# Splitting the tokens' high and low parts over three steps, and the closing sums behind one convolution step

## Chip, cores and metric

One core of one Trainium2 chip. The time is device time in microseconds (us) of one launch; below it is the median of three runs of the kernel before. TensorE is PE (its weight loads are PEld), VectorE DVE, ScalarE ACT, GpSimd POOL, SyncE SP.

## The reference

A convolution whose seven taps are drawn per token and head by a softmax, and behind it a feed-forward layer with squared relu:

```python
w = exp(weight_gen - max(weight_gen, -1)); w = w / (sum(w, -1) + 1e-9)   # B S 8 7
x_pad = concatenate([zeros(6 rows), x], axis=1)                          # x: 8 x 4096 x 192
attn = einsum('bshk,bskhg->bshg', w, x_pad[:, s + k])                    # 24 columns a head
h = attn.reshape(32768, 192) @ w_in                                      # 192 x 2048
out = (maximum(h, 0) ** 2) @ w_out                                       # 2048 x 192
```

x and weight_gen are float32; w_in and w_out come as float64 and are decoded by the kernel.

## The kernel before, in words

**Tiling.** The 32768 tokens lie 256 to a partition; a chunk is 4 tokens of each partition, 512 tokens, so there are 64 chunks. For a chunk, DVE makes the softmax and the seven products and adds of the convolution (`conv_steps`, lines 326 to 500), turns the result with a 32 x 32 transpose (L487), and SP sends it through memory (`xr` to `xd` with four DMAs, L493, `xd` to `xT` with two, L498), so that the 192 columns stand on partitions. `xT` has three parts of 512 columns, one for each third of the 192.

**Precision.** PE multiplies in a reduced float32 form. Each operand is therefore split into a high part, rounded by a copy on ACT (`high_part`, L427, `xT` to `xh`; `high`, L550, `rg` to `gh`), and a low part, the rest, by a subtraction on DVE (`low_part`, L430, to `xl`; `low`, L559 and L562, to `gl`).

**Steps.** A chunk is worked in eight steps j (the loop at lines 878 to 932). In step j PE multiplies the tokens by 2 of the 16 column blocks of W (`mm1`, L522: nine products for each block, in the order xh for the three parts, xl for the three parts, xh with W's low part), ACT does relu (L539), square (L546) and the high half (L550), and DVE does the low half one step later (`late`). Two steps behind (LAG) PE multiplies the finished blocks by V (`mm2_scaled`, L603 and L607) into four PSUM banks. Every product is done in two halves of 64 rows, which PE's array runs side by side. After the last block of a chunk come 32 small products (L613), and the chunk's sums are closed: `sum_turned` copies one half's bank by ACT (L648) and adds the other half's by DVE (L650), part 0 and then part 1. Only then may the next chunk's L603 products write these banks. The closing of chunk c - 1 stands in step 1 of chunk c, its banks are wanted again in step 2.

**Chunks 6 to 62** are "scaled": x and V are scaled by powers of two, so that the low halves `gl` can be kept in float16 (`V16` is V's float16 copy, kept with part of `gl` in the tile `du`). The factors come from the peaks of W and V (`peak_w`, `peak_v`), which `spread_peaks` (lines 299 to 304) sends to memory and back to all partitions with two DMAs, and from which `coefficients` computes eight numbers. `scale_v` (lines 321 to 324) scales V in place.

**Order.** Each engine works its instructions in the order in which they are written here. `at(c, j, f)` puts f into the list `todo` of step j of chunk c; entries made before the loop stand first. The convolution of chunk m begins in step 1 of chunk m - 2: SCALED_SLOTS says how many of its 19 steps go to each of ten successive steps of the loop; the last, `turn`, falls in step 2 of chunk m - 1. The splits of chunk m are put into steps 5 and 6 of chunk m - 1 (lines 856 and 857). Where a step closes a chunk, N_AHEAD entries of its list come before the closing sums (lines 908 to 927). In step 1 the list holds the last product and the last add of the next chunk's convolution and the maximum and the subtraction of the softmax of the chunk after it.

Of the kernel before, what the change touches and what calls it, by code (L numbers as in the profile page):

```python
# [8 lines left out]
F32 = mybir.dt.float32  # L9
# [4 lines left out]
AF = mybir.ActivationFunctionType  # L14
ALU = mybir.AluOpType
# [15 lines left out]
def kernel(  # L31
# [9 lines left out]
    nc = tc.nc  # L41
    B, S, D = x.shape
# [3 lines left out]
    P = 128  # L46
# [10 lines left out]
    ND = D // D1  # L57
    N = TC * P
    NJ = NF // 2
# [3 lines left out]
    LAG = 2  # L63
    CONV_BEG = 1
    CONV_SLOTS = (2, 1, 4, 1, 3, 0, 3, 3, 0, 3)
    SCALED_SLOTS = (2, 1, 4, 1, 2, 1, 3, 2, 2, 1)
    OUT_STEP = 3
    LOAD_STEP = 5
    NBUF = NF // 2
    FIRST = 6  # L70
    GL_POOL = 5
    SCALE_STEP = NJ
    N_AHEAD = 2

    const = ctx.enter_context(tc.tile_pool(name="const", bufs=1))
    stage = ctx.enter_context(tc.tile_pool(name="stage", bufs=3))
# [33 lines left out]
    def is_scaled(c):  # L110
        return FIRST <= c < NCH - 1
# [7 lines left out]
    V = const.tile([P, NF, 2 * D], F32R, name="V")  # L119
    du = const.tile([P, 4, 2 * WI], U32, name="du")  # L120
    du_flat = du.rearrange("p a b -> p (a b)")
    V16 = du_flat[:, 0:NF * D // 2].bitcast(F16).rearrange("p (f e) -> p f e", f=NF)
# [3 lines left out]
    tops = du_flat[:, NF * D // 2:NF * D // 2 + 2 * P].bitcast(F32)  # L126
    coef = const.tile([P, 8], F32, name="coef")
    w_mul, v_mul, v_root, v_unroot = (coef[:, k:k + 1] for k in range(4))
# [39 lines left out]
    def load_rest():  # L168
        t0 = rows_of(0)
        wf = w_tiles[0].rearrange("p t h k -> p t (h k)")  # L170
        nc.sync.dma_start(out=wf[:, TC:, :], in_=wg_v[:, t0 + TC:t0 + TG, :])
        nc.sync.dma_start(out=x_tiles[0][:, HALO + TC:, :], in_=x_v[:, t0 + TC:t0 + TG, :])
# [73 lines left out]
    def dec(u, *idx, half=None):  # L246
        if u not in decs:
            decs[u] = decode_steps(u)
        i0, i1 = (0, 2) if half is None else (half, half + 1)
        for n in idx:  # L250
            decs[u](n, i0, i1)
            if n == 3 and i1 == 2 and u + 3 < 2 * NU:
                load_weights(u + 3)
                if u == 1:
                    load_rest()
# [43 lines left out]
    def spread_peaks():  # L299
        dm = dram.tile([P, 2], F32, name="dm")  # L300
        pk = coef[:, 4:6]
        nc.vector.tensor_reduce(out=pk, in_=peaks.rearrange("p (w k) -> p w k", w=2), axis=AX.X, op=ALU.max)
        nc.sync.dma_start(out=dm, in_=pk)
        nc.sync.dma_start(out=tops, in_=dm.rearrange("p w -> (p w)").rearrange("(o n) -> o n", o=1).broadcast_to([P, 2 * P]))

    def coefficients():
        ts = nc.vector.tensor_scalar
# [10 lines left out]
        ts(out=v_root.bitcast(U32), in0=v_root.bitcast(U32), scalar1=POW2, scalar2=None, op0=ALU.bitwise_and)  # L318
        nc.vector.tensor_tensor(out=v_mul, in0=v_root, in1=v_root, op=ALU.mult)

    def scale_v(j):
        v = V[:, 2 * j:2 * j + 2]
        nc.vector.tensor_scalar(out=v, in0=v.bitcast(F32), scalar1=v_mul, scalar2=None, op0=ALU.mult)
        nc.scalar.copy(V16[:, 2 * j:2 * j + 2], v[:, :, 0:D].bitcast(F32))

    def conv_steps(c, on_pe, moving=False):
        gi, lo = divmod(c, CPG)
# [2 lines left out]
        n = TC * H  # L330
# [74 lines left out]
        def both(*fs):  # L405
            return lambda: [f() for f in fs]
# [25 lines left out]
        def split(k):  # L432
            return both(lambda: high_part(k), lambda: low_part(k))

        splits = [split(k) for k in range(ND)]
        if moving and not on_pe:
            splits = [[lambda f=f, k=k: f(k) for k in range(ND)] for f in (high_part, low_part)]

# [109 lines left out]
    def high(c, fb):  # L548
        gh = ghs[c, fb] = gp.tile([P, N], F32R, name="gh")
        nc.scalar.copy(gh, rgs[c, fb])  # L550

    def low(c, fb):
        if is_scaled(c):
            j, i = divmod(fb, 2)
            if i == 0:
                gls[c, j] = gp.tile([P, 2, N], F16, name="gl") if j < GL_POOL else gl_rest[:, j - GL_POOL]
            gl = gls[c, j][:, i].rearrange("p (m i) -> p i m", i=2)
            g, h = (v.rearrange("p (i m) -> p i m", i=2) for v in (rgs.pop((c, fb)), ghs[c, fb].bitcast(F32)))
            nc.vector.tensor_tensor(out=gl, in0=g, in1=h, op=ALU.subtract)  # L559
            return  # L560
        gl = gls[c, fb] = gp.tile([P, N], F32R, name="gl")
        nc.vector.tensor_tensor(out=gl, in0=rgs.pop((c, fb)), in1=ghs[c, fb].bitcast(F32), op=ALU.subtract)  # L562
# [79 lines left out]
    def sum_turned(c, parts=(1, 0)):  # L642
        acc = accs[c]
        if c not in works:
            works[c] = stage.tile([P, 3, N], F32, name="raw")
        X = works[c]
        for k in parts:
            nc.scalar.copy(X[:, k], acc[2 * k])  # L648
        for k in parts:
            nc.vector.tensor_tensor(out=X[:, k], in0=acc[2 * k + 1], in1=X[:, k], op=ALU.add)  # L650
        if 1 in parts and is_scaled(c):
            nc.gpsimd.dma_start(out=X[0:D1, 1], in_=X[D1:P, 1], accum_op=ALU.add)  # L652
        elif 1 in parts:
            nc.sync.dma_start(out=X[0:D1, 2], in_=X[D1:P, 1])
# [57 lines left out]
    def store(c, t0, t1):  # L712
        put_out(c, t0, t1, outs[c][0], 1 if c == 0 else 0)
# [44 lines left out]
    done = iter(range(NF))  # L758
# [68 lines left out]
    todo, soon, pend, late = {}, {}, [], []  # L827

    def at(c, j, f):
        todo.setdefault((c + j // NJ, j % NJ), []).append(f)  # L830
# [5 lines left out]
    def plan_conv(m, a, b):  # L836
        if m == 3:
            for f in a[:2]:
                at(1, 1, f)
            soon[1, 2] = a[2:3]  # L840
            spread(a[3:], 1, 3, 3 + NJ)
        elif m > 3:
            fs = iter(a)
            for j, n in enumerate(SCALED_SLOTS if is_scaled(m) else CONV_SLOTS):
                for _ in range(n):
                    at(m - 2, CONV_BEG + j, next(fs))
        else:
            for j, fs in enumerate(((), a[4:5], a[5:8], a[8:])):
                for f in fs:
                    at(1, j, f)  # L850
        if m < 2 + CPG:
            soon[m - 1, NJ - 1] = b[0] + b[1][:ND * (m == 2)]
            for f in b[1][ND * (m == 2):]:
                at(m - 1, NJ - 1, f)
        else:
            for k, f in enumerate(b):
                at(m - 1, NJ - 3 if k == 0 and is_scaled(m) else NJ - 2, f)

    for k in range(4):
        at(2, k + 3, lambda k=k: peak_v(k))  # L860
        at(3, k, lambda k=k: peak_w(k))
    at(3, 4, spread_peaks)
    at(3, 7, coefficients)
    for j in range(NJ):
        at(FIRST - 1, j + 4, lambda j=j: scale_v(j))
    for gi in range(FIRST // CPG, NCH // CPG):
# [7 lines left out]
    plan_conv(3, *conv_steps(3, 0, True))  # L874
    for u in range(1, NU):
        at(1, 2 * u, lambda u=u: dec(NU + u, 5))

    for c in range(1, NCH):
        tail = c == NCH - 1
        for j in range(NJ):  # L880
            if j == (LOAD_STEP if c > 1 else 0) and c % 2 and (c + 3) // 2 * CPG < NCH:
                load_group((c + 3) // 2)
            if j == CONV_BEG and 1 < c < NCH - 2:
                plan_conv(c + 2, *conv_steps(c + 2, 0))
            if c == 1 and j == 0:
                mm1(c, j, (0, 1, 6, 7, 3, 4, 2, 8, 5), 5)
            else:
                mm1(c, j)
            fbs = (2 * j, 2 * j + 1)
            done = None  # L890
            if len(pend) == LAG or tail and pend:
                c2, j2 = pend.pop(0)
                for fb in (2 * j2, 2 * j2 + 1):
                    mm2_turned(c2, fb)
                done = c2 if j2 == NJ - 1 else None
            for f in soon.pop((c, j), []):
                f()
            for fb in fbs:
                relu(c, fb)
            for fb in fbs:  # L900
                square(c, fb)
            if not tail:
                pend.append((c, j))
            for f in late:
                f()
            late.clear()
            fs = todo.pop((c, j), [])
            split_sum = done is not None and is_scaled(done)
            if split_sum:
                for f in fs[:N_AHEAD]:  # L910
                    f()
                del fs[:N_AHEAD]
                sum_turned(done, (0,))
            elif done is not None:
                sum_turned(done)
            for f in fs:
                f()
            if c > 1:
                for part in range(2):
                    if j == (LOAD_STEP if tail else 2 * part + 2 if is_scaled(c - 1) else OUT_STEP + part):  # L920
                        store_turned(c - 1, part)
            if not tail or j < NJ // 2:
                for fb in fbs:
                    high(c, fb)
                    late.append(lambda c=c, fb=fb: low(c, fb))
            if split_sum:
                sum_turned(done, (1,))
            if c == 1 and j == 0:
                for t in range(TC // 2):
                    finish(0, t)  # L930
            if c == 1 and j == NJ - 1:
                store(0, 0, TC)
    c = NCH - 1
# [56 lines left out]
```

## Time and profile before

| | |
|---|---|
| median of 3 runs | 2102.3 us (2101.99 to 2102.64) |
| profiled execution | 2101.76 us |
| its span, first to last instruction | 2100.0 us |
| granted TensorE clock, mean | 0.998 of 2.4 GHz |
| busy | PE 2074.4, PEld 1707.0, DVE 1870.8, ACT 1845.2, POOL 221.2 us |

The profile is of one execution. A busy time counts the union of an engine's instructions; matmuls overlap each other, so PE's share says little of its peak. An idle time is put down to the instruction that released the engine.

### The profile page before, as it was taken

The numbers are of one execution on the slowest core, as the hardware profiler recorded it, in microseconds if no ns is written. First come the engines' busy times: TensorE is split into PE (matmuls) and PEld (weight loads), VectorE is DVE, ScalarE is ACT, GpSimd is POOL, SyncE is SP. The second block draws the span as 40 slices with busy tenths as digits, with TensorE's granted clock in tenths as the row PEclk, the third lists the DMA queues.
The fourth block names the chain that finished last, engine by engine and source line by source line (L and its number), as shares of the span: only waits on it lengthen the run. The fifth ranks groups of instructions, "written<-read, shape, count | busy, mean of one in ns | idle before, by whom it ended". The sixth has DMA issues, their size and how long they took to land.

```text
span 2100.0 us, 49532 instructions
## 1 busy us (share of the span) xinstructions
PE 2074.4 (99%) x19484; PEld 1707.0 (81%) x19484; DVE 1870.8 (89%) x2953; ACT 1845.2 (88%) x3551; POOL 221.2 (11%) x364
## 2 busy tenths in 40 slices
PE   9999999999999999999999999999999999999999
PEld 8887878878888788888888788787788878888878
DVE  9989899898898898998988988989889889999885
ACT  8887988889888899889898888998888988988986
POOL 0000110111110111101111101111011110011110
PEclk9999999999999999999999999999999999999999
DMA  9524454534545445445355354354453553544522
GB/s 234 101 51 98 108 117 97 122 73 105 125 97 110 93 91 118 113 98 121 70 110 126 94 113 93 90 120 106 104 120 71 110 125 93 116 85 97 122 59 56
DMA packets 322289, 217.78 MB, mean 104 GB/s; under 512 B 215696, under 2 KB 273168, under 8 KB 318216
## 3 DMA queue, kind: packets, MB, share of 16 engines
q1 hardware_dynamic: 300568, 181.17, 37.3%
q0 software_dynamic: 21488, 33.46, 9.4%
q8 instruction: 152, 2.49, 0.5%
q14 instruction: 81, 0.66, 0.1%
HBM read 106.52 MB, written 49.55 MB: 74 GB/s over the span
## 4 chain that ended last, share of the span: by engine, by line
PE 71%; DVE 15%; DMA 6%; ACT 4%; issue 2%; SPq 1%; DVEq 0%; ACTq 0%
PE ph L522 38%; PE acc L603 21%; DMA xT<-xd 4%; PE acc L607 4%; PE acc L613 4%; DVE pr L384 4%; DVE du L559 3%; DVE pr L397 3%; PE acc L638 3%; DVE xl L430 2%; DVE raw L650 1%; DVE gl L559 1%; ACT rg L539 1%; PE acc L570 1%; ACT rg L546 1%
## 5 line engine op out<-in xcount | busy, mean ns | idle before, releaser
L522 PE MATMUL ph<-xh,W 64*128 64x512 f32 x6096 | 1069.0, 403 | 0.0
L522 PEld LDWEIGHTS ph<-xh,W 64*128 64x128 f32 x6096 | 718.3, 186 | 100.9 <-ACT gh L550 23.0
L603 PE MATMUL acc<-gh,V 64*128 64x512 f32 x5472 | 772.9, 378 | 10.1 <-DVE raw L650 8.4
L539 ACT ACTIVATE rg<-ph 128x512 f32<-128x512 f32 x992 | 539.0, 596 | 197.8 <-PE ph L522 193.1
L603 PEld LDWEIGHTS acc<-gh,V 64*128 64x128 f32 x5472 | 594.4, 186 | 104.1 <-DVE raw L650 32.2
L546 ACT ACTIVATE rg<-rg 128x512 f32<-128x512 f32 x1007 | 580.5, 634 | 0.2
L550 ACT CAST gh<-rg 128x512 fp32r<-128x512 f32 x1008 | 576.1, 626 | 3.0 <-PE acc L580 3.0
L522 PE MATMUL ph<-xl,W 64*128 64x512 f32 x3048 | 495.3, 376 | 0.1
L559 DVE TENSOR_TENSOR gl<-rg,gh 128x512 f16<-128x512 f32 x570 | 389.6, 740 | 47.4 <-ACT gh L550 47.4
L384 DVE TENSOR_TENSOR pr<-xt,wt 128x768 f32<-128x768 f32 x440 | 412.3, 949 | 2.3
L522 PEld LDWEIGHTS ph<-xl,W 64*128 64x128 f32 x3048 | 361.5, 186 | 40.4 <-ACT xl L441 0.5
L397 DVE TENSOR_TENSOR pr<-pr 128x768 f32<-128x768 f32 x309 | 295.2, 955 | 6.1
L559 DVE TENSOR_TENSOR du<-rg,gh 128x512 f16<-128x512 f32 x342 | 232.0, 732 | 3.7 <-ACT gh L550 3.7
L607 PE MATMUL acc<-gl,du 64*128 64x512 f16 x1140 | 230.8, 381 | 1.0 <-DVE gl L559 1.0
L430 DVE TENSOR_TENSOR xl<-xT,xh 128x512 fp32r<-128x512 f32 x186 | 122.2, 687 | 122.0 <-ACT xh L427 121.8
L652 POOL DMA_DIRECT2D raw<-raw x57 | 47.3, 830 | 1261.3 <-DVE raw L650 1170.6
L607 PEld LDWEIGHTS <-du 64*128 64x128 f16 x1824 | 101.7, 95 | 62.3 <-issue 4.7
L607 PE MATMUL acc<-du 64*128 64x512 f16 x684 | 138.2, 382 | 0.0
L285 POOL DMA_DIRECT2D x_out<-x_fac x232 | 112.3, 493 | 42.5 <-DVE x_fac L282 41.4
L427 ACT CAST xh<-xT 128x512 fp32r<-128x512 f32 x186 | 108.1, 619 | 9.3 <-DMA xT<-xd 8.6
L402 POOL DMA_DIRECT2D pr<-pr x63 | 57.0, 905 | 531.3 <-DVE pr L384 484.8
L613 PEld LDWEIGHTS <-du 64*64 64x64 f16 x1824 | 48.3, 106 | 57.9 <-issue 24.1
(127 smaller groups left out, 1267.7 us busy)
## 6 DMA issues: line engine op xcount, KB each, us to landing
xT<-xd SPq DMA_DIRECT2D x124, 384.0 KB
xt<-in_x_dram SPq DMA_DIRECT2D x30, 1344.0 KB
out_dram<-o_sb SPq DMA_DIRECT2D x254, 96.0 KB
pr<-pr POOLq DMA_DIRECT2D x63, 384.0 KB, 5.8
xd<-xr SPq DMA_DIRECT2D x248, 96.0 KB
o_sb<-raw SPq DMA_DIRECT2D x342, 64.0 KB
raw<-raw POOLq DMA_DIRECT2D x57, 128.0 KB, 3.9
wt<-in_weight_gen_dram SPq DMA_DIRECT2D x31, 224.0 KB
```

Source lines behind the costliest of these rows:

```text
L285: nc.gpsimd.dma_start(out=fo[b * P // n:(b + 1) * P // n], in_=f[b::n])
L384: tt(out=dst, in0=src, in1=wf[:, t0 * H:t1 * H, k:k + 1].broadcast_to([P, m, G]), op=ALU.mult)
L397: tt(out=prs[k0], in0=prs[k0], in1=prs.pop(k), op=ALU.add)
L430: tt(out=parts["l"][:, k, n], in0=src[k][:, n], in1=parts["h"][:, k, n].bitcast(F32), op=ALU.subtract)
L522: nc.tensor.matmul(two[i], w, order(xx[rows, k]), start=(n == 0), stop=(n == last))
L539: nc.scalar.activation(r, ph, AF.Relu)
L546: nc.scalar.activation(r, r, AF.Square)
L550: nc.scalar.copy(gh, rgs[c, fb])
L559: nc.vector.tensor_tensor(out=gl, in0=g, in1=h, op=ALU.subtract)
L603: nc.tensor.matmul(acc[b + h], V[rows, fb, e:e + P], two_halves(g[rows]), start=fb == 0 and e < 2 * P, stop=False)
L607: nc.tensor.matmul(acc[h], V16[rows, 2 * j + i, 0:P], gls[c, j][rows, i], start=False, stop=last and i == 1)
L613: nc.tensor.matmul(acc[2 + h][i * D1:(i + 1) * D1], V16[rows, 2 * k + i, P:D], gls[c, k][rows, i], start=False, stop=k == NJ - 1, tile_pos ...
```

## The change

The splits of a scaled chunk m: in step 5 of chunk m - 1 the high parts 0 and 1, in step 6 the low parts 0 and 1 and the high part 2, in step 7 the low part 2 (before: high and low 0 in step 5, high and low 1 and 2 in step 6). SCALED_SLOTS moves convolution steps accordingly: step 5 takes one more, step 7 one less, and step 6 a product in place of an add. In a closing step of a scaled chunk one convolution step is ahead of the sums in place of two, and the two sums stand together, with only the high halves (ACT) between; the rest of the list follows. The DMAs of `spread_peaks` are issued by POOL two steps later, `coefficients` is three steps later, in chunk 4. V's float16 copies are made straight from the unscaled V in chunk 4, alternately on DVE and ACT, and the scaling in place in chunks 5 and 6 alternates likewise.

```diff
-    SCALED_SLOTS = (2, 1, 4, 1, 2, 1, 3, 2, 2, 1)
+    SCALED_SLOTS = (2, 1, 4, 1, 3, 1, 2, 2, 2, 1)
-    N_AHEAD = 2
+    N_AHEAD = 1
@@ spread_peaks
-        nc.sync.dma_start(out=dm, in_=pk)
-        nc.sync.dma_start(out=tops, in_=dm.rearrange(...).broadcast_to([P, 2 * P]))
+        nc.gpsimd.dma_start(out=dm, in_=pk)
+        nc.gpsimd.dma_start(out=tops, in_=dm.rearrange(...).broadcast_to([P, 2 * P]))
@@
+    def scaled_copy(j, o, i):
+        if j % 2:
+            nc.scalar.activation(o, i.bitcast(F32), AF.Copy, scale=v_mul)
+        else:
+            nc.vector.tensor_scalar(out=o, in0=i.bitcast(F32), scalar1=v_mul, scalar2=None, op0=ALU.mult)
+
+    def make_v16(j):
+        scaled_copy(j, V16[:, 2 * j:2 * j + 2], V[:, 2 * j:2 * j + 2, 0:D])
+
     def scale_v(j):
         v = V[:, 2 * j:2 * j + 2]
-        nc.vector.tensor_scalar(out=v, in0=v.bitcast(F32), scalar1=v_mul, scalar2=None, op0=ALU.mult)
-        nc.scalar.copy(V16[:, 2 * j:2 * j + 2], v[:, :, 0:D].bitcast(F32))
+        scaled_copy(j, v, v)
@@ conv_steps
+        if is_scaled(c):
+            splits = [(lambda k=k: high_part(k), lambda k=k: low_part(k)) for k in range(ND)]
@@ plan_conv
-            for k, f in enumerate(b):
-                at(m - 1, NJ - 3 if k == 0 and is_scaled(m) else NJ - 2, f)
+            for f in b if not is_scaled(m) else ():
+                at(m - 1, NJ - 2, f)
+            for k, (f, g) in enumerate(b if is_scaled(m) else ()):
+                at(m - 1, NJ - 3 + k // 2, f)
+                at(m - 1, NJ - 2 + k // 2, g)
@@
-    at(3, 4, spread_peaks)
-    at(3, 7, coefficients)
+    at(3, 6, spread_peaks)
+    at(4, 2, coefficients)
+    for j in range(NJ):
+        at(4, 3 + j // 2, lambda j=j: make_v16(j))
@@ the loop of steps
+            if split_sum:
+                highs_of(c, fbs)
+                sum_turned(done, (1,))
             for f in fs:
                 f()
...
-            if not tail or j < NJ // 2:
-                for fb in fbs:
-                    high(c, fb)
-                    late.append(lambda c=c, fb=fb: low(c, fb))
-            if split_sum:
-                sum_turned(done, (1,))
+            if not split_sum and (not tail or j < NJ // 2):
+                highs_of(c, fbs)
```

`highs_of` holds the loop over `high` and `late.append` that stood here.

## Rows read from the trace of the kernel before

**Rows 1.** The page: engines' busy time; line L430 (busy us, mean ns | idle before).

```profile
PE 2074.4 (99%) x19484; PEld 1707.0 (81%) x19484; DVE 1870.8 (89%) x2953; ACT 1845.2 (88%) x3551; POOL 221.2 (11%) x364
...
L430 DVE TENSOR_TENSOR xl<-xT,xh 128x512 fp32r<-128x512 f32 x186 | 122.2, 687 | 122.0 <-ACT xh L427 121.8
```

**Rows 2.** PEld in order of time (start us, us, instruction), chunks 62 and 63.

```profile
2035.32 0.51 PEld L522 LDWEIGHTS ph<-xh,W 64*128 64x128 f32 x6 [0.41 <-ACT gh L550]
...
2038.89 0.62 PEld L522 LDWEIGHTS ph<-xh,W 64*128 64x128 f32 x6
...
2061.00 0.62 PEld L522 LDWEIGHTS ph<-xh,W 64*128 64x128 f32 x6
...
2066.84 0.51 PEld L522 LDWEIGHTS ph<-xh,W 64*128 64x128 f32 x6 [0.41 <-ACT gh L550]
```

**Rows 3.** PEld in order of time, chunk 6 step 2 and chunk 7 step 3.

```profile
231.06 0.62 PEld L522 LDWEIGHTS ph<-xh,W 64*128 64x128 f32 x6
...
271.60 0.83 PEld L522 LDWEIGHTS ph<-xh,W 64*128 64x128 f32 x6
```

**Rows 4.** PEld in order of time, chunk 30, steps 1 to 3.

```profile
1000.98 0.83 PEld L522 LDWEIGHTS ph<-xh,W 64*128 64x128 f32 x6
...
1007.03 0.51 PEld L522 LDWEIGHTS ph<-xh,W 64*128 64x128 f32 x6 [0.41 <-ACT gh L550]
...
1009.88 0.73 PEld L603 LDWEIGHTS acc<-gh,V 64*128 64x128 f32 x7 [0.39 <-DVE raw L650]
...
1010.87 0.83 PEld L522 LDWEIGHTS ph<-xh,W 64*128 64x128 f32 x6
```

**Rows 5.** The waits view (engine line <- releaser: us in total, times, longest).

```profile
PEld acc L603 <- DVE raw L650: 32.2, 59, 1.0
...
DVE coef L309 <- DMA du<-dm: 9.0, 1, 9.0
...
ACT xh L427 <- DMA xT<-xd: 8.6, 22, 0.9
```

**Rows 6.** DVE in order of time, closings in chunk 30 and in chunk 62.

```profile
1006.95 0.96 DVE L397 TENSOR_TENSOR pr<-pr 128x768 f32<-128x768 f32 x1
...
1009.14 0.68 DVE L650 TENSOR_TENSOR raw<-acc,raw 128x512 f32<-128x512 f32 x1
...
1011.05 0.98 DVE L487 STREAM_TRANSPOSE xr<-pr 128x768 f32<-128x768 f32 x1
...
2036.04 0.69 DVE L650 TENSOR_TENSOR raw<-acc,raw 128x512 f32<-128x512 f32 x1 [0.60 <-ACT raw L648]
2036.65 1.38 DVE L559 TENSOR_TENSOR gl<-rg,gh 128x512 f16<-128x512 f32 x2
```

**Rows 7.** PEld and SP's queue in order of time, chunks 3 and 4.

```profile
151.21 0.64 PEld L522 LDWEIGHTS ph<-xh,W 64*128 64x128 f32 x6
...
165.45 0.62 PEld L522 LDWEIGHTS ph<-xh,W 64*128 64x128 f32 x6
...
149.93 0.54 SPq L303 DMA_DIRECT2D dm<-coef  x1
152.79 0.34 SPq L304 DMA_DIRECT2D du<-dm  x1
```

**Rows 8.** Groups of instructions by line: scaling and copying of V.

```profile
L323 DVE TENSOR_SCALAR V<-V,coef 128x768 fp32r<-128x768 f32 x8 | 4.9, 611 | 0.0
...
L324 ACT CAST du<-V 128x384 f16<-128x384 f32 x8 | 4.1, 510 | 4.6 <-DVE V L323 4.5
```

**Rows 9.** ACT and PEld in order of time, chunk 30 step 5 to chunk 31.

```profile
1022.66 0.62 ACT L427 CAST xh<-xT 128x512 fp32r<-128x512 f32 x1
...
1027.32 1.15 ACT L550 CAST gh<-rg 128x512 fp32r<-128x512 f32 x2
...
1029.94 0.83 PEld L522 LDWEIGHTS ph<-xl,W 64*128 64x128 f32 x6
```

**Rows 10.** The page's DMA issues: POOL's accumulating DMA (KB each, us to landing).

```profile
pr<-pr POOLq DMA_DIRECT2D x63, 384.0 KB, 5.8
```

More of the change, by code (lines that the diff above doesn't have):

```diff
@@ L302, in spread_peaks @@
         nc.vector.tensor_reduce(out=pk, in_=peaks.rearrange("p (w k) -> p w k", w=2), axis=AX.X, op=ALU.max)
-        nc.sync.dma_start(out=dm, in_=pk)
-        nc.sync.dma_start(out=tops, in_=dm.rearrange("p w -> (p w)").rearrange("(o n) -> o n", o=1).broadcast_to([P, 2 * P]))
+        nc.gpsimd.dma_start(out=dm, in_=pk)
+        nc.gpsimd.dma_start(out=tops, in_=dm.rearrange("p w -> (p w)").rearrange("(o n) -> o n", o=1).broadcast_to([P, 2 * P]))
     def coefficients():
@@ L876, with highs_of @@
         at(1, 2 * u, lambda u=u: dec(NU + u, 5))
+    def highs_of(c, fbs):
+        for fb in fbs:
+            high(c, fb)
+            late.append(lambda fb=fb: low(c, fb))
     for c in range(1, NCH):
```

## The prediction

> **What bounds the kernel now.** I read the page first: PE is busy 99% of the span, DVE and ACT 89% and 88% [rows 1]. A busy PE says nothing of how close its work is packed, so the next view was the order of time on PE's weight loads, where a step of the loop shows as the start of its first W load (L522). A chunk is eight such steps. From step 2 of chunk 62 to step 2 of chunk 63 PE waits for nobody: 2066.84 - 2035.32 = 31.52 us [rows 2]. That is six plain steps of 3.685 (2038.89 to 2061.00), a closing step of 5.84 (2061.00 to 2066.84, with the 32 small L613 products) and a step of 3.57 behind it (2035.32 to 2038.89). The 55 chunks from 271.60 to 2038.89 take 1767.29 us, 32.13 each [rows 2, 3]. So PE loses 0.61 us a chunk, 33.7 us in all.
>
> Where it loses them shows in chunk 30 [rows 4]. The closing step takes 6.05 (1000.98 to 1007.03), the step behind it 3.84 (1007.03 to 1010.87). In that second step PE starts the next chunk's L603 products and is held until DVE has added the second closing sum (L650): five of twelve weight loads go, the other seven wait. The waits view has this 59 times, 32.2 us [rows 5]. The wait also leaves the two 64-row halves of the array one slot apart: afterwards six W loads take 0.83 us, where chunk 62 shows 0.62 [rows 2, 4]. I read the 0.21 us by which 6.05 exceeds 5.84 as the price of that skew, paid when the next closing has to bring the halves together.
>
> The sum is late because DVE stands in a queue: in step 1 it does product, add (0.96), first closing sum, maximum, subtraction and only then the second sum, at 1009.14, 2.11 us after PE's step 2 began [rows 6]. In chunk 62, where there is no softmax left to start, the same sum begins at 2036.04, 0.72 behind PE's step, waiting only for ACT's copy, and PE does not stop [rows 2, 6].
>
> Two one-time losses precede this. In chunk 4, PE's step from 151.21 to 165.45 takes 14.24 in place of 4.10, 10.1 lost [rows 7]: DVE waits 9.0 for the spread peaks [rows 5], which SP could issue only at 149.93, behind a run of o_sb stores [rows 7]. And from 231.06 (chunk 6, step 2) to 271.60 (chunk 7, step 3) PE takes 40.54 [rows 3], where seven plain steps, a closing and the step behind it make 25.8 + 5.84 + 3.57 = 35.2: 5.3 lost while ACT waits for DVE's scaling of V to copy each part (4.5 in all) [rows 8].
>
> **The change, part by part.** *Closing sums.* With one convolution step ahead of them, DVE does the product, the first sum and the second sum; the add, the maximum and the subtraction come behind. ACT's order is the same (copy, two high halves, copy). The second sum can start when ACT's copy has ended, 0.72 behind PE's step, as in chunk 62; that pattern showed no wait. I take the whole 33.7: about 22 from the wait itself (3.84 and its longer cases to 3.57) and 11.6 from the skew (55 x 0.21). Bounds: nothing of the skew (22), or all.
>
> What is queued behind: the second sum starts at 0.72 and takes 0.61 (2036.04 to 2036.65); add, maximum and subtraction take 1.58 (1006.95 to 1009.14 without the first sum's 0.61); two gl subtractions 1.26 (the pair's 1.38 less the overlap of two neighbours). So the transpose (L487) starts at 4.17, where chunk 30 shows 1011.05 - 1007.03 = 4.02 [rows 4, 6]. PE reaches step 5 another 0.27 sooner (3.57 for 3.84). So the turned tokens (xT, over SP's four and two DMAs, which no other transfer newly precedes) land 0.42 to 0.45 later against PE's steps. ACT today waits for them 22 times, 8.6 us in all, 0.9 at most, at no cost [rows 5].
>
> *High and low parts.* The same three ACT copies and three DVE subtractions per chunk; two copies now stand in step 5, and the subtractions in steps 6, 6 and 7. DVE's waits behind the first copy (121.8 us over the run) go [rows 1], and so does DVE's lateness at the closing. But the last subtraction now stands behind the two gl subtractions of step 6, and these need ACT's high halves. In chunk 30 ACT starts the first copy at 1022.66 and those halves at 1027.32 [rows 9]; the same instructions lie between after the change, in another order. So: first half done 1027.95, two gl subtractions to 1029.2 (pitch 0.63, from the pair's 1.38 [rows 6]), last low part 0.69 [rows 1], ready at 1029.9. PE loads weights for that part two pairs after 1029.94, at 1030.37 [rows 9]. **The margin is 0.46 us**, where today both last parts are done before step 0 begins. Each microsecond by which xT is later than in this chunk, above 0.46, is a microsecond of PE. With the shift of 0.45 the margin is used up just where ACT waits today: 8.6 us come back. DVE itself is full from step 3 to step 7 in chunks that measure the tokens' power (ACT's halves are late there), which I put at 0.1 in 27 chunks, 3. **Sum 12 us back**; bounds: 0 if the landings spread as favourably as in the best chunks, 25 if the shift counts in all 55 chunks (55 x 0.45).
>
> The moved convolution steps (an add to step 5, a product to step 6) are DVE work in DVE's own order; the product in step 6 needs a buffer that POOL's accumulating DMA frees. That DMA is issued in step 4, not quite two steps (7.4) ahead of the product's new place, and lands in 5.8 [rows 10]: about 1 us of cover, and if it is gone the same third low part is late, within the 25.
>
> *Peaks and coefficients.* The small reduction moves two steps later (8.2), to about 145.7, its two DMAs to POOL's queue, to which the convolutions of chunks 4 and 5 give nothing, so that nothing stands ahead. On SP the second DMA was issued 2.86 after the first, which it had waited for [rows 7], and the reading of the coefficients ran some 4 after that; POOL's large DMAs take 5.8 [rows 10]. So two of them land between 152.6 (145.7 + 6.9) and 157.3 (145.7 + 11.6). DVE comes to the coefficients in step 2 of chunk 4, which PE would begin at 151.21 + 4.10 = 155.3 and DVE, working about a step behind, reaches near 159. No wait: the 10.1 go. SP's queue loses a wait (for dm) in front of further stores. *V.* The half-precision copies (8, of 0.51 [rows 8]) move to chunk 4, half of them to DVE, which costs at most 0.61 each (twice the width) [rows 8]; chunk 4 has steps of 4.10 and both engines have room. The scaling of chunk 5 is shared: DVE drops 4 x 0.61, ACT does 4 of some 1.0 (twice the 0.51; bounds 0.61 and 1.2) in place of 8 x 0.51 and waits for nobody. Of 5.3 I take 4.8; bounds 2 and 5.3.
>
> **Sum**, against the profiled execution's 2101.76 (the median is 0.5 above): 2101.76 - 33.7 - 10.1 - 4.8 + 12 = 2065.2, as a median 2065.7; I say **2066**.
>
> **Rivals.**
> 1. *The low part is hidden after all.* Then nothing comes back: 2054. For it: 37 of 59 chunks have no wait of ACT for xT today [rows 5]. Against: the margin of 0.46 and the shift of 0.45. Chance 0.14.
> 2. *The skew is not the closing wait's.* Then the closing step stays at 6.05 and 11.6 of the 33.7 stay: 2077. For it: one closing (chunk 63's) is my witness. Against: the 0.62 and 0.83 rows. Chance 0.11.
> 3. *The peaks are late on POOL's queue too.* DVE stands at the coefficients with the gl subtractions and closing work behind it; all 10 lost again at worst: 2076. For: POOL must write the descriptors itself while DVE runs. Against: POOL's accumulating DMAs, of 384 KB, land in 5.8 beside a DVE that is 89% busy [rows 1, 10]. Chance 0.06. The Trainium skill ("GPSIMD Engine Reference", Specifications) says POOL's SBUF interface is shared with VectorE and contends with its two-input instructions, and "DMA: Bandwidth & Descriptors" (Issuing engine by pattern) gives simple loads to SyncE; by those two the transfer would be the slower one and the time this rival's 2076. No row here shows such a contention.
> 4. *Slower: the last low part holds PE in every chunk by more than the closing gave.* Place: step 0 of each chunk, third xl weight load. It costs what xT is late above the margin; the gains of 48.6 are gone at 48.6 / 55 = 0.88 a chunk, that is with xT 1.3 later than in chunk 30; at 1.0 a chunk the time is 2108. Against: the longest wait today is 0.9. Chance 0.03; half way there, 2078 to 2098, 0.08.
> 5. *The change does not do what it says*: ACT's second copy is held, so the second sum stays late, and low parts still cost: about 2097 to 2100. ACT's order is unchanged, so 0.02.
>
> **How the numbers follow.** The forecast with its bounds (2057 to 2074) has the rest, 0.56. A measurement of this kernel tells 0.2%, 4.2 us, from no change. The range reaches down to rival 1 and up past rivals 2 and 3 into the first part of 4: 2053 to 2086, leaving out some 0.12. Faster by over 0.2% are all cases but the end of rival 4 and rival 5: 0.94; same 0.03; slower 0.03.
>
> **What would show it.** Right: step 1 to step 2 of a chunk at 5.84 and step 2 at 3.57; six W loads in 0.62 all through; the second L650 0.7 behind step 2, with idle time that ACT's copy ends; ACT waiting for xT in most chunks; PE's weight loads of L522 idle behind L430 at step 0, some tenths in a third to half of the chunks; no wait of L309; chunk 4 without its 14.24. Wrong: waits behind L430 near 1 us in most chunks, 6.05 unchanged, or DVE idle at L309.

## The result, and the profile after

The changed kernel takes 2075.3 us (median of 4, 2072.8 to 2078.2) where the kernel before takes 2102.1: a ratio of 0.987 (95% interval 0.986 to 0.989), 27 us faster. The forecast was 2066, its range 2053 to 2086. The profiled execution took 2076.22 us, its span 2074.1.

Lines have moved. W's loads and products are L532 (before L522), the splits L435 and L438 (L427, L430), the products with V L613 (L603), the small ones L623 (L613), the two halves of a closing sum L658 on ACT and L660 on DVE (L648, L650), the turn L497, `xd` L503, `xT` L508.

First PE's weight loads in order of time (start us, us, instruction), chunk 30, steps 1 to 3, then the ends of the 55 chunks 8 to 62. They answer to [rows 2 to 4].

```profile
986.30 0.62 PEld L532 LDWEIGHTS ph<-xh,W 64*128 64x128 f32 x6
...
990.29 1.44 PEld L623 LDWEIGHTS <-du 64*64 64x64 f16 x32 [0.42 <-issue]
992.14 0.51 PEld L532 LDWEIGHTS ph<-xh,W 64*128 64x128 f32 x6 [0.41 <-ACT gh L560]
...
993.98 1.27 PEld L613 LDWEIGHTS acc<-gh,V 64*128 64x128 f32 x12
...
995.72 0.62 PEld L532 LDWEIGHTS ph<-xh,W 64*128 64x128 f32 x6
...
285.10 0.62 PEld L532 LDWEIGHTS ph<-xh,W 64*128 64x128 f32 x6
...
2031.29 0.62 PEld L532 LDWEIGHTS ph<-xh,W 64*128 64x128 f32 x6
```

The closing step takes 5.84 (986.30 to 992.14), the step behind it 3.58 (to 995.72); the twelve L613 loads go in one run, and six W loads take 0.62 all through. This is the forecast's picture of a closing, in every chunk from 8 on. Yet the 55 chunks take 1746.19 us (285.10 to 2031.29), 31.75 each and not 31.52: 12.5 us are lost elsewhere.

The waits view says where (engine line <- releaser: us in total, times, longest), beside [rows 5].

```profile
PEld ph L532 <- DVE xl L438: 15.0, 17, 2.5
...
ACT xh L435 <- DMA xT<-xd: 25.9, 34, 2.7
...
DVE raw L660 <- ACT raw L658: 71.7, 92, 2.1
```

PE has no wait for DVE's sum left, and DVE now waits for ACT's half of that sum. PE waits for the low part instead, 17 times, 15 of them in chunks 8 to 62; ACT waits for the tokens 34 times (22 before), up to 2.7 us (0.9 before).

The whole run, cut at the first W load of each chunk (us; a chunk without a loss takes 32.81 while unscaled, 31.52 scaled, chunk 6, where the two meet, some 30.3):

| | to chunk 2 | chunk 4 | chunk 6 | chunk 7 | chunks 8 to 62 | rest | span |
|---|---|---|---|---|---|---|---|
| before | 81.31 | 42.94 | 33.97 | 33.19 | 1767.29 | 141.29 | 2099.99 |
| after | 82.75 | 38.30 | 31.24 | 34.19 | 1746.20 | 141.41 | 2074.09 |
| change | +1.44 | -4.64 | -2.73 | +1.00 | -21.09 | +0.12 | -25.90 |

The first column is no part of the change: over all kernels shown here it lies between 81.2 and 85.6.

In chunk 4 the peaks are in time: POOL issues them at 146.63 and 151.63, and DVE reads the coefficients at 163.75 without a wait. But step 4 of that chunk takes 9.45 (165.11 to 174.56) in place of 4.10. The order of time on PE's loads, SP's queue and ACT:

```profile
165.11 0.62 PEld L532 LDWEIGHTS ph<-xh,W 64*128 64x128 f32 x6
...
170.31 0.19 PEld L648 LDWEIGHTS acc<-gh,V 64*128 64x128 f32 x2 [3.28 <-ACT gh L560]
...
174.56 0.62 PEld L532 LDWEIGHTS ph<-xh,W 64*128 64x128 f32 x6
...
139.79 16.04 SPq L690 DMA_DIRECT2D o_sb<-raw  x23
...
159.54 0.42 SPq L157 DMA_DIRECT2D xt<-in_x_dram  x1
...
166.61 1.48 ACT L270 ACTIVATE du<-xt 128x1536 bf16<-128x1536 f32 x1 [5.38 <-DMA xt<-in_x_dram]
```

Read from below: ACT stands 5.4 us at the measurement of group 3's tokens, because SP issues their load only at 159.54, behind 16 us of stores into `o_sb` and 3 us of output stores. PE then lacks ACT's high half for 3.3 us. The step is 5.35 too long; PE waits 3.28 and 0.54 of it, and the rest goes at a lower granted clock. This is the stretch up to the next step (columns: busy time of PE, PEld, DVE, ACT and POOL, granted clock, DMA share, GB/s):

```profile
170.30:174.50 4.20, 3.95 (x18) 3.01 (x20) 3.99 (x11) 4.20 (x9) 0.00 (x0) 0.59 0.47 102
```

One long wait for the low part, in step 0 of chunk 23, by PE's loads and SP's queue, and by stretches (columns as above):

```profile
758.06 0.41 PEld L532 LDWEIGHTS ph<-xh,W 64*128 64x128 f32 x4
758.94 0.18 PEld L532 LDWEIGHTS ph<-xh,W 64*128 64x128 f32 x2 [0.48 <-ACT xh L435]
...
761.41 0.19 PEld L532 LDWEIGHTS ph<-xl,W 64*128 64x128 f32 x2 [1.95 <-DVE xl L438]
...
762.70 2.42 PEld L613 LDWEIGHTS acc<-gh,V 64*128 64x128 f32 x12
...
765.59 0.62 PEld L532 LDWEIGHTS ph<-xh,W 64*128 64x128 f32 x6
```

```profile
741.31 1.83 SPq L503 DMA_DIRECT2D xd<-xr  x4
746.91 1.29 SPq L508 DMA_DIRECT2D xT<-xd  x2
...
808.19 1.81 SPq L503 DMA_DIRECT2D xd<-xr  x4
811.73 1.29 SPq L508 DMA_DIRECT2D xT<-xd  x2
```

```profile
758.00:761.40 3.40, 1.78 (x14) 0.87 (x10) 3.23 (x6) 3.40 (x8) 0.00 (x0) 1.00 0.02 5
761.40:764.90 3.50, 3.49 (x18) 2.76 (x20) 3.50 (x6) 3.11 (x8) 0.00 (x0) 0.53 0.00 0
```

The step takes 7.53 (758.06 to 765.59), 3.85 too long. PE waits 0.48 + 1.95; the other 1.4 go behind the wait, where the granted clock is 0.53, close to the lower level of 1.2 GHz, and twelve L613 loads take 2.42 for 1.27. The tokens were late: SP could issue `xT` only 5.6 us after the first `xd` store (741.31 to 746.91), two chunks later 3.5 (808.19 to 811.73). The steps of step 0 that are over 0.15 too long stand in ten chunks, and chunks 23, 31, 39, 47 and 55, eight apart, hold 10.55 of the 12.5 us.

### The profile page after: what moved, and what is told of

Same layout as the page of the kernel before. It is cut to its first block, busy times and chain, and to the rows that moved or that the text cites. A ratio compares the mean times of both kernels' runs of the same rounds, so it can differ in the third digit from the quotient of the medians.

```text
span 2074.1 us, 49551 instructions
## 1 busy us (share of the span) xinstructions
PE 2054.8 (99%) x19484; PEld 1621.0 (78%) x19484; DVE 1873.6 (90%) x2953; ACT 1840.6 (89%) x3551; POOL 222.2 (11%) x366
## 4 chain that ended last, share of the span: by engine, by line
PE 84%; ACT 5%; DMA 3%; DVE 3%; issue 1%; SPq 1%; POOL 0%; ACTq 0%; DVEq 0%; POOLq 0%
PE ph L532 42%; PE acc L613 25%; PE acc L617 9%; PE acc L623 5%; PE acc L648 3%; DMA xT<-xd 2%; ACT gh L560 1%; ACT rg L549 1%; ACT rg L556 1%; SPq L690 1%; PE acc L590 1%; DVE du L569 1%; DMA xt<-in_x_dram 1%; DMA pr<-pr 0%; ACT du L270 0%
## 5 line engine op out<-in xcount | busy, mean ns | idle before, releaser
L532 PE MATMUL ph<-xh,W 64*128 64x512 f32 x6096 | 909.5, 403 | 0.1
L532 PEld LDWEIGHTS ph<-xh,W 64*128 64x128 f32 x6096 | 578.5, 186 | 135.6 <-ACT gh L560 23.4
L613 PE MATMUL acc<-gh,V 64*128 64x512 f32 x5472 | 666.7, 376 | 0.0
L613 PEld LDWEIGHTS acc<-gh,V 64*128 64x128 f32 x5472 | 519.6, 186 | 72.5 <-ACT gh L560 0.2
L532 PE MATMUL ph<-xl,W 64*128 64x512 f32 x3048 | 418.1, 377 | 9.7 <-DVE xl L438 9.3
L532 PEld LDWEIGHTS ph<-xl,W 64*128 64x128 f32 x3048 | 291.5, 186 | 54.7 <-DVE xl L438 15.0
L617 PE MATMUL acc<-gl,du 64*128 64x512 f16 x1140 | 173.4, 381 | 0.3 <-DVE gl L569 0.2
L660 DVE TENSOR_TENSOR raw<-acc,raw 128x512 f32<-128x512 f32 x124 | 85.3, 691 | 72.4 <-ACT raw L658 71.7
L617 PEld LDWEIGHTS <-du 64*128 64x128 f16 x1824 | 53.6, 95 | 109.9 <-issue 109.5
L435 ACT CAST xh<-xT 128x512 fp32r<-128x512 f32 x186 | 108.4, 619 | 26.1 <-DMA xT<-xd 25.9
L438 DVE TENSOR_TENSOR xl<-xT,xh 128x512 fp32r<-128x512 f32 x186 | 121.0, 681 | 2.3 <-ACT xh L435 2.3
L285 POOL DMA_DIRECT2D x_out<-x_fac x232 | 112.4, 494 | 85.6 <-DVE x_fac L282 82.2
L617 PE MATMUL acc<-du 64*128 64x512 f16 x684 | 103.7, 382 | 0.0
```

What stands on the lines that cost most here:

```text
L285: nc.gpsimd.dma_start(out=fo[b * P // n:(b + 1) * P // n], in_=f[b::n])
L435: nc.scalar.copy(parts["h"][:, k, n], src[k][:, n])
L438: tt(out=parts["l"][:, k, n], in0=src[k][:, n], in1=parts["h"][:, k, n].bitcast(F32), op=ALU.subtract)
L532: nc.tensor.matmul(two[i], w, order(xx[rows, k]), start=(n == 0), stop=(n == last))
L613: nc.tensor.matmul(acc[b + h], V[rows, fb, e:e + P], two_halves(g[rows]), start=fb == 0 and e < 2 * P, stop=False)
L617: nc.tensor.matmul(acc[h], V16[rows, 2 * j + i, 0:P], gls[c, j][rows, i], start=False, stop=last and i == 1)
```

## The experiments

**Each part of the change alone.** e1: the kernel before with the new order of the closing only.

```diff
-    N_AHEAD = 2
+    N_AHEAD = 1
+            if split_sum:
+                highs_of(c, fbs)
+                sum_turned(done, (1,))
             for f in fs:
```

> The kernel before with the new closing order alone (one convolution step ahead of the sums, the sums together). Theory A: PE's loss is the second closing sum standing behind an add, a maximum and a subtraction. The sum then starts about 0.75 us behind PE's step 2, the chunk takes 31.52 us (closing step 5.84, the step behind it 3.57), 33.7 us go in 55 chunks and 1.7 in chunk 7: 2067 us. The low parts are where they were and have over 2 us of margin, so no wait of PE for xl; chunk 4 keeps its 14.24 us step. Rival B: what makes the sum late is DVE's waiting for the first high part in step 5, and the order at the closing matters little: the step behind the closing stays near 3.84, about 2098 us.

2091.6 us, ratio 0.994 (0.993 to 0.996). Theory A has fallen: chunks 8 to 62 take 1758.23, 9.1 us of the 33.6 that there were to win. Its waits:

```profile
PEld acc L603 <- DVE raw L650: 23.8, 55, 0.9
...
DVE xl L430 <- ACT xh L427: 162.5, 61, 3.9
...
ACT xh L427 <- DMA xT<-xd: 80.3, 55, 2.8
```

PE still waits for the second sum 55 times, now in 28 of the 55 chunks (54 before), mostly twice in one, and once in chunk 6. The third row is the price: the convolution's last add and the turn behind the sums are later, so is `xT`, ACT waits for it in 54 of the 55 chunks, and DVE, whose low part stood right behind that copy, waits 162.5 us (121.8 before [rows 1]). DVE comes to the closing later than it did: it begins the last product ahead of the sums 5.8 us behind PE's step 1, before the change 5.0 (medians of the 55 chunks). So the second sum, with less ahead of it, begins only 0.2 sooner, 1.95 behind step 2 in place of 2.13.

e2: the kernel before with the splits in steps 5 to 7 and the new SCALED_SLOTS only; the order of the closing stays.

```diff
-    SCALED_SLOTS = (2, 1, 4, 1, 2, 1, 3, 2, 2, 1)
+    SCALED_SLOTS = (2, 1, 4, 1, 3, 1, 2, 2, 2, 1)
...
-                at(m - 1, NJ - 3 if k == 0 and is_scaled(m) else NJ - 2, f)
+                at(m - 1, NJ - 3 + k // 2, f)
+                at(m - 1, NJ - 2 + k // 2, g)
```

> The kernel before with the splitting of the tokens and the convolution slots alone; at the closing add, first sum, maximum, subtraction and second sum stay in the old order. In the changed kernel DVE idles 1.26 us a chunk before the sums, and add, maximum and subtraction take 1.58. Theory A (it is lateness that counts, not order): DVE comes early enough that the second sum starts near 1.05 us behind PE's step 2, PE wants the bank at 2.26, so 31.52 us a chunk as well; the transpose starts 1.3 us sooner than in the changed kernel, so xT is in time and PE waits for xl in no chunk: 2067 us. Rival C (the order at the closing is what the gain needs): the step behind the closing stays at 3.8 or above, and the low part's waits come on top: 2095 to 2110 us.

2069.2 us, 0.984 (0.982 to 0.985). Chunks 8 to 62 take 1733.69, 31.52 each, the whole of it. Theory A holds and Rival C falls. Its closing in chunk 30, in the order of DVE (the sum is L652 there), and DVE's wait behind the first copy:

```profile
995.92 0.96 DVE L397 TENSOR_TENSOR pr<-pr 128x768 f32<-128x768 f32 x1
996.79 0.68 DVE L652 TENSOR_TENSOR raw<-acc,raw 128x512 f32<-128x512 f32 x1
997.40 0.38 DVE L353 TENSOR_REDUCE mx<-wt 128x32 f32<-128x224 f32 x1
997.81 0.39 DVE L354 TENSOR_TENSOR wt<-wt,mx 128x224 f32<-128x224 f32 x1
998.12 0.68 DVE L652 TENSOR_TENSOR raw<-acc,raw 128x512 f32<-128x512 f32 x1
...
DVE xl L430 <- ACT xh L427: 3.4, 2, 2.3
```

PE's step 2 begins at 997.35 there. The second sum starts 0.77 later with add, maximum and subtraction still ahead of it; in [rows 6] it was 2.11. DVE is not late any more: the 121.8 us of waiting are 3.4, and it begins the last product 3.6 behind step 1 (5.0 before, medians as above). So the split earns the closing's gain, and the new order isn't needed for it. The three moved convolution steps of SCALED_SLOTS came with the split and were not tried apart from it. ACT's wait for `xT` in this kernel is 1.1 us in 3 times, and no low part is late from chunk 8 on.

e3: the one-time part only (peaks, coefficients, V).

```diff
-        nc.sync.dma_start(out=dm, in_=pk)
+        nc.gpsimd.dma_start(out=dm, in_=pk)
...
-    at(3, 4, spread_peaks)
-    at(3, 7, coefficients)
+    at(3, 6, spread_peaks)
+    at(4, 2, coefficients)
+    for j in range(NJ):
+        at(4, 3 + j // 2, lambda j=j: make_v16(j))
```

> The kernel before with the later peaks, coefficients and copies of V alone. Theory A: chunk 4 loses 5.3 us in place of 10.1 (ACT then waits for the x of chunks 6 and 7, whose load SP issues behind the stores of chunk 2), chunks 6 and 7 lose about 2 in place of 5.3 (the closing of chunk 6 stays): 2094 us. Rival: the 5.3 us in chunk 4 belong to POOL's transfer of the peaks, then DVE waits at L309; or all of chunk 4's loss goes with the old splits: 2089 us.

2098.6 us, 0.997 (0.996 to 0.9985); chunk 4 takes 38.56, where 32.81 would lose nothing. The peaks' wait is gone and the load's has come:

```profile
ACT du L270 <- DMA xt<-in_x_dram: 6.8, 2, 5.7
```

e4: the changed kernel with the old order of the closing.

```diff
-    N_AHEAD = 1
+    N_AHEAD = 2
-            if split_sum:
-                highs_of(c, fbs)
-                sum_turned(done, (1,))
             for f in fs:
```

> The changed kernel with the old order at the closing (two convolution steps ahead, maximum and subtraction between the sums). Theory A: as in the split alone, 31.52 us a chunk without waits of PE for xl (the transpose starts 1.3 us sooner), so the 15 us of waits for xl go and nothing comes back: 2059 us. Rival C: the step behind the closing goes back to 3.84 and the closing step to 6.05, some 30 us more, less what the xl waits give: 2090 us.

2063.2 us, 0.980 (0.979 to 0.982): 12 us faster than the change as it stands.

```profile
ACT xh L435 <- DMA xT<-xd: 1.8, 4, 0.8
```

ACT's 25.9 us of waiting for the tokens are 1.8. In chunk 22 `xd` is issued at 740.16, 7.3 before step 5, against 5.7 in the changed kernel: the new order's add and turn behind the sums are what makes the tokens late. One late low part is left in chunks 8 to 62 (chunk 45, 1.6). Chunk 4 still loses 7.3, to the load as in e3.

**The load of group 3.** e5: the changed kernel with that load in step 2 of chunk 3.

```diff
-            if j == (LOAD_STEP if c > 1 else 0) and ...
+            if j == (2 if c == 3 else LOAD_STEP if c > 1 else 0) and ...
```

> The changed kernel with one thing moved: the load of tokens and taps of group 3 is issued in step 2 of chunk 3 in place of a later step, so that on SP's queue it stands ahead of the unscaled o_sb stores. Theory F (the 5.3 us lost in step 4 of chunk 4 are that load's, issued at 159 behind 24 stores): step 4 of chunk 4 falls from 9.44 to below 5, and the time from 2075.3 to about 2070. Rival G (the step is lost to DVE's and ACT's work in chunk 4, the copies of V among it, and the load only happens to end beside it): step 4 stays above 8, the time at 2075. Rival H (SP now waits for the buffer in step 2 and holds the stores behind it): the loss moves to chunk 3, the time at 2075 or above.

2069.1 us, 0.985 (0.983 to 0.986). Theory F holds: chunk 4 takes 32.81.

```profile
125.58 0.44 SPq L157 DMA_DIRECT2D xt<-in_x_dram  x1
...
137.86 16.31 SPq L690 DMA_DIRECT2D o_sb<-raw  x24
```

e6: the diffs of e4 and e5 together.

> The changed kernel with the old order of the closing (two convolution steps ahead of the first sum, the others between the sums) and the load of group 3 in step 2 of chunk 3. Theory F: the gain of the early load, about 5 to 7, adds to the gain of the old order (2063.2): about 2057, with one or two waits for the last low part in chunks 8 to 62. Rival G (the load costs nothing by itself): 2063.

2058.5 us, 0.979 (0.978 to 0.981), 1.5 above what was expected. Chunks 8 to 62 lose 0.5, chunk 4 nothing. Chunk 7 loses 4.24 in step 0, in place of 2.67: a wait of 2.25 for the last low part, and here too a lower clock behind it.

```profile
247.21 0.29 PEld L532 LDWEIGHTS ph<-xl,W 64*128 64x128 f32 x2 [2.25 <-DVE xl L438]
...
248.00:251.30 3.30, 3.30 (x24) 2.36 (x22) 3.27 (x6) 2.46 (x5) 0.00 (x0) 0.63 0.18 25
```

**Why every eighth chunk?** PE runs 608 instructions a chunk (144 + 96 + 32 + 32 products, and as many loads), and the profile's page has a queue that brings instructions:

```profile
q8 instruction: 152, 2.49, 0.5%
```

That is 16.4 KB for each of 152 packets, and 38968 PE instructions in 152 packets are 256 each; eight chunks are 19 packets exactly. e7 adds 16 matmuls (32 instructions) ahead of all work, e8 adds 8.

```diff
-    for _ in range(9):
+    for _ in range(25):  # e7
+    for _ in range(17):  # e8
```

> The changed kernel with 16 more dummy matmuls ahead of all work, 32 PE instructions more, the rest word for word. Theory K (the long waits for the last low part, in chunks 23, 31, 39, 47, 55, come from the transfer of PE's own instructions, one 16 KB packet for 256 instructions, 608 instructions a chunk, so with a period of 8 chunks, which meets the tokens' DMAs): the long waits move to other chunks, to 12, 20, 28 and so on, 8 apart; their sum stays 8 to 16 and the time within 4 of 2075. Rival L (the period is that of loads and stores of data, or of DVE's and ACT's work): the long waits stay in chunks 23, 31, 39, 47, 55.

2077.8 us, 0.988 (0.987 to 0.990). The long waits have moved: 9, 17, 25, 33, 41, 49 and 57 lose about 1 each (0.96 to 1.63), chunks 12, 20, 36, 44 and 60 some 0.2 to 0.8, and the sum is 12.1. Theory K holds in that the period stays and the place moves, and Rival L falls; of the chunks named only the smaller group was right. What the late chunks share is the place of one packet. The DMA view of the changed kernel from 743.5 to 747, ahead of chunk 23:

```profile
q8 instruction: 1, 0.02, 3.0%
```

The same view of e7 from 555 to 558, ahead of chunk 17, and there the order of time on SP, ahead of chunk 17 and of chunk 23 (which loses 0.48 now):

```profile
q8 instruction: 1, 0.02, 2.8%
```

```profile
553.33 1.81 SPq L503 DMA_DIRECT2D xd<-xr  x4
558.55 1.29 SPq L508 DMA_DIRECT2D xT<-xd  x2
...
743.63 1.81 SPq L503 DMA_DIRECT2D xd<-xr  x4
747.34 1.29 SPq L508 DMA_DIRECT2D xT<-xd  x2
```

In both kernels the packet starts 7.8 to 7.9 us behind step 2 (743.85 and 555.95), takes 1.7 and 1.3 us, and falls while the `xd` stores are under way; `xT` is issued 5.2 to 5.6 us after the first `xd`. The trace's start times of all packets give the same picture for chunks 8 to 62: in the changed kernel 13 chunks have a packet within 3.5 us behind their first `xd` store, and `xT` follows that store by 4.3 to 5.6 us in 12 of them (3.8 in chunk 15), by 3.5 to 4.0 in the other 42; in e7 it is 4.1 to 5.9 in 14 chunks and 3.5 to 4.2 in 41. Only those with the longest delays cost PE much. In e4 such delays are as long (4.5 to 5.5 us in 14 chunks), but its stores start 1.3 to 1.6 us sooner, and only chunk 45 loses. That the packet holds up one engine's share of the stores is inferred from this, since the trace does not say which engine carried what.

> The changed kernel with 8 more dummy matmuls ahead of all work, 16 PE instructions more. Theory K: each instruction packet comes about 0.85 us earlier against the steps (16 instructions of some 53 ns each), partly clear of the tokens' transfers: the waits in chunks 23, 31, 39, 47, 55 fall from 10.5 us together to below 5, the time by 4 to 9, to 2066 to 2071; or, if 0.85 us is too little, the waits stay in those chunks and only change their sizes. Rival L: chunks and sizes as before, 2075.

2073.1 us, 0.986 (0.985 to 0.988): the waits stay in the same eighth chunks (15, 23, 31, 39, 47, 55) and sum to 6.6, and chunk 28 loses 1.25. Theory K's second branch. The packets came sooner by more than the 0.85 expected (ahead of chunk 23 the packet starts 6.1 behind step 2, in place of 7.8), but still among the stores. A packet 2.9 to 3.4 behind the first `xd` store delays nothing in six chunks of this run and delays chunk 28, so the place decides, and not wholly. By itself this run doesn't tell K from L.

**The last low part.** e9: the changed kernel with it in step 6.

```diff
                 at(m - 1, NJ - 3 + k // 2, f)
-                at(m - 1, NJ - 2 + k // 2, g)
+                at(m - 1, NJ - 2, g)
```

> The changed kernel with the last low part put into step 6, directly behind its high part and so ahead of the two gl subtractions that DVE makes there, in place of step 7. Theory M (PE waits in step 0 because the last low part stands behind those two subtractions, 1.26 us, and their high halves): each wait shrinks by 1.26 or more; the waits below 0.6 are gone, those of chunks 23, 31, 39, 47 and 55 (1.32 to 3.85) keep 0 to 1 each, some 3 together in place of 12.5, chunk 7 keeps 1.4 of 2.67, and the time is about 2064. Rival N (DVE, now waiting for ACT's third high part in step 6, comes late to the closing, as before the change): no wait in step 0, but the step behind the closing grows from 3.58 by 0.1 to 0.3 and the time is 2070 or above.

2061.5 us, 0.980 (0.9785 to 0.982). Theory M is right and was modest: the waits in chunks 8 to 62 fall from 12.5 to 0.7, chunk 7's from 2.67 to 0.58. Rival N is there too, but small: in chunks 7, 15, 23, 39 and 47 the step behind the closing is 0.13 to 0.23 too long. These rows show more, chunk 15 and the closing after it:

```profile
512.39 0.51 PEld L532 LDWEIGHTS ph<-xh,W 64*128 64x128 f32 x6 [0.41 <-ACT rg L556]
...
515.21 0.73 PEld L613 LDWEIGHTS acc<-gh,V 64*128 64x128 f32 x7 [0.36 <-DVE raw L660]
...
538.30 0.83 PEld L532 LDWEIGHTS ph<-xh,W 64*128 64x128 f32 x6
...
544.35 0.52 PEld L532 LDWEIGHTS ph<-xh,W 64*128 64x128 f32 x6 [0.41 <-ACT gh L560]
544.89 0.62 PEld L532 LDWEIGHTS ph<-xl,W 64*128 64x128 f32 x6
```

The wait at 515.21 leaves six loads at 0.83 until the next closing, which takes 6.05 (538.30 to 544.35) and sets them back to 0.62. The five closings of 6.05 in this kernel (chunks 8, 16, 24, 40, 48) each come in the chunk behind such a wait; the others take 5.84 but one (5.94 in chunk 32).

e10: e6 with group 4's load in step 2 of chunk 5 as well.

```diff
-            if j == (2 if c == 3 else LOAD_STEP if c > 1 else 0) and ...
+            if j == (2 if c in (3, 5) else LOAD_STEP if c > 1 else 0) and ...
```

> The changed kernel with the old order of the closing and the loads of groups 3 and 4 in step 2 of chunks 3 and 5. In the version with group 3 alone, ACT still waits 1.34 for group 4's tokens in chunk 6 and DVE behind it 1.45, and chunk 7's step 0 is 4.24 too long: 2.67 of waiting for the last low part and 1.57 at a lower granted clock. Theory P (the wait for the load makes DVE late through chunk 6): the wait falls to about 1.2, with no clock drop, and chunk 6 to 30.3; the time is 2058.5 less 3 to 3.5, about 2055. Rival Q (DVE has more work in chunk 6 than fits, with the scaling of V and the last unscaled sums, and would be as late without that wait): chunk 7's step 0 stays at 6.3 or above, the time at 2057 or above.

2058.7 us, 0.979 (0.978 to 0.981), as e6. Theory P was half right: ACT's wait for the load is gone and chunk 6 takes 30.38, but chunk 7's step 0 is 4.19 too long as before, as Rival Q said. The tokens of chunk 7 are late by themselves: `xd` is issued 3.5 before step 5 (7.3 in the chunks after). What holds the turn there, the closing of an unscaled chunk in step 1 or V's scaling, was not tried.

e11: the diffs of e6 and e9 together.

> The changed kernel with three edits together: the old order of the closing, the load of group 3 in step 2 of chunk 3, and the last low part in step 6. Theory M: the early last low part takes chunk 7's step 0 from 7.9 to about 4.3, as it did with the new order of the closing, and chunk 45's wait of 0.5 goes, while the chunks from 8 on stay at 31.52: 2058.5 less 4, about 2054.5. Rival N: with tokens that land early DVE's wait for ACT's third high part costs something at the closing, steps behind it above 3.58, and the time is 2058 or above.

2056.3 us (2055.9 to 2057.4), 0.9775 (0.976 to 0.979), the lowest ratio of all, though its interval overlaps e6's. Chunk 7 takes 33.18 in place of 35.76; 1.1 us of that loss has moved into its step 2. Chunks 8 to 62 take 1735.03 (e6: 1734.21), with the closing's wait back in a few late chunks: Rival N's mechanism, at 0.8 us.

## Why the prediction was right and wrong

The sign, the range and the likeliest case held; the median was missed by 9.3 us, the profiled time by 11 (2065.2 against 2076.2). By the prediction's own steps:

- **Closing sums, 33.7.** The size was right: e2 shows 33.6 (1767.29 less 1733.69), and the skew went with the wait, as e9's rows show, so the second rival is dead. The part that earns it was named wrong: the order alone wins 9.1 (e1), the split alone all of it (e2). That the sum came out even so is luck, since the same change held the split, which the prediction had down as a cost. The step that failed is "that pattern showed no wait". Chunk 62, the witness, lacks more than the softmax, as DVE's rows of before show beside chunk 30's first sum:

```profile
1007.82 0.68 DVE L650 TENSOR_TENSOR raw<-acc,raw 128x512 f32<-128x512 f32 x1
...
2019.55 0.69 DVE L430 TENSOR_TENSOR xl<-xT,xh 128x512 fp32r<-128x512 f32 x1 [2.29 <-ACT xh L427]
...
2033.49 1.38 DVE L559 TENSOR_TENSOR gl<-rg,gh 128x512 f16<-128x512 f32 x2
2034.77 0.67 DVE L650 TENSOR_TENSOR raw<-acc,raw 128x512 f32<-128x512 f32 x1
```

No product and no add stand ahead of its first sum, though DVE waited 2.29 for the split there as in other chunks. So DVE begins that sum 0.55 ahead of PE's step 2 (2034.77 to 2035.32), in chunk 30 0.79 behind it (1007.03 to 1007.82): the witness showed a DVE that is on time, which the split brings about and the order by itself does not. The row was in the prediction's hands: 121.8 us of DVE's waits behind the first copy [rows 1], to which it gave half a sentence and no microsecond.
- **Low part, 12 back.** Measured 12.5 in chunks 8 to 62, and 2.67 in chunk 7. That the numbers agree is in good part luck: not some tenths in a third to half of the chunks, but 10.55 of the 12.5 in five, at the places of the instruction packets, with a lower clock in one; in none of the five did ACT wait in the kernel before, and 8.6 of the 12 were worked out from its waits there. The shift of 0.45 was sound: DVE's turn starts 6.7 before step 5, 7.2 before the change (medians). But the order puts the turn 1.3 to 1.6 later than the old one does with the same splits (5.7 for 7.0 to 7.3 before step 5), and e4 shows what that costs, 12 us (10.9 of it in chunks 8 to 62). The prediction took the old kernel's late turn as its base, and so did not see that the split alone would have bought the time that the order spends.
- **Chunk 4, 10.1.** 4.64. The step that failed: "No wait: the 10.1 go". The wait it looked at did go; what was late next was group 3's load on SP, behind the same stores that had delayed the peaks, and a lower clock behind that wait. The trace of before has the load at 162.03 on SP's queue, where the stop for the peaks covered it. e3 and e5 show it. It is 5.5 of the 11.
- **Chunks 6 and 7, 4.8.** 1.73 (2.73 less 1.00). ACT's wait for V is gone; chunk 7's late low part brings 2.67 back, with the split alone too (e2's chunk 7 takes 34.19 as well), and the prediction had no such term. Also, 1.65 of its 5.3 lay in chunk 7's step 2 (5.23 for 3.58), where the split and not V's scaling helps: 5.60 in e3, 3.57 in e2. The two chunks are 3.1 of the 11.
- **The start**, 1.44 of the 11, varies between kernels that are the same up to there; 0.6 more lie in chunks 8 to 62 (21.1 won for 21.7), the rest is small.
- **Rivals.** Peaks late on POOL (2076) named nearly the time that came, by a cause that did not occur. The Trainium skill ("DMA: Bandwidth & Descriptors", Issuing engine by pattern) gives simple loads to SyncE; the trace agrees so far: POOL took longer from the first issue to the second, 5.0 (146.63 to 151.63) against 2.9 on SP [rows 7]. It cost nothing, since DVE reads them 12 us later. Rivals 1, 4 and 5 are excluded by the waits view.

## What to carry to other kernels

An engine that is late at one place was made late at another: before reordering the place where it hurts, look for that engine's largest wait earlier in the loop, and test each half of a change alone. When a wait on a shared queue is taken away, read on down the same queue, since the next transfer behind the same stores takes its place. A margin of a few tenths of a microsecond isn't kept by the median landing but by the worst, so move what need not stand ahead of the consumer out of its way.

## What was not expected of the hardware

- Instructions come in packets of 16 KB, which the profile counts in the share of the core's 16 DMA engines, 0.9 to 2.2 us each in the changed kernel. That these are PE's is inferred from their number and from e7. A short chain of transfers that meets one is up to some 2 us late, with a period of eight chunks in this loop.
- After waits of 1.95 and 2.25 us (chunk 23 here, chunk 7 in e6) the granted clock was 0.53 to 0.63 for some 3.5 us, which cost 1.4 to 1.6 (the step's excess less the waits in chunk 23, and less the 2.67 of the changed kernel in e6). After the 3.28 of chunk 4 it was 0.59. A wait of 2.47 in chunk 7 of the changed kernel was followed by none:

```profile
254.80:257.30 2.50, 2.50 (x26) 1.93 (x26) 2.50 (x4) 2.38 (x5) 0.00 (x0) 1.00 0.14 20
```

So the wait's length alone did not decide it, and what does is left open.
- A wait that divides PE's twelve L613 loads into five and seven leaves six W loads at 0.83 us for a whole chunk, and the next closing takes 0.21 longer (e9). That PE's two 64-row halves are then one slot apart is how these rows are read; the trace doesn't show it directly.
